# Sixty-one preferences in a planner's order of an attention and Fourier-mixing kernel

## The chip, the cores and the metric

One NeuronCore of a Trainium2 chip runs the whole kernel. The metric is the device time of one execution in microseconds; the median of three runs of the kernel before is 265.67 us (264.87 to 266.83). The profile is of a single execution with a span of 263.2 us.

## The reference

Two parts follow each other. The first is attention over q, k, v of 4 batches, 8 heads, 768 positions and 64 features, with 8 global keys, a causal window of 96 keys and a linear distance bias per head:

```python
scores = scale * np.matmul(q, k.transpose(0, 1, 3, 2))
is_global = pos[None, :] < int(n_global)
is_local = (rel >= 0) & (rel < int(n_local))
bias = -slopes[:, None, None] * dist[None, :, :]
scores = np.where(is_global | is_local, scores + bias, -1e9)
a = softmax(scores); out = a @ v
```

The heads are put side by side to x of shape (4, 768, 512), and the second part is

```python
X = np.fft.fft(np.fft.fft(x, axis=1), axis=2)
u = x + np.real(X)
un = (u - mu) / np.sqrt(var + 1e-06)          # over the last axis
return u + np.maximum(un @ w_ch1, 0.0) @ w_ch2
```

with w_ch1 of 512 x 2048 and w_ch2 of 2048 x 512. (Both are shortened here; names are the reference's.)

## The kernel before

The work is cut into units, and each unit is a function that emits instructions. A unit of TensorE is a group of matmuls into one PSUM bank or bank pair; what follows on the other engines (casts, exponentials, copies out of PSUM, folds, loads, stores) are single operations.

**Units of TensorE** stand in four lists. A unit's name is a pair (list, place).
- List 0, MIX, has ten units for each batch: four first transforms `py` (L979) of the folded attention output, three second transforms `pu` (L1059), and three transposes `ptu` (L1150) of normalized rows.
- List 1, ATT, has the attention. For batch 0: (1,0) ones, (1,1) transpose of the first head pair's q and k (`pt`, L575), (1,2) to (1,4) its scores (`sc`, a bias product L621 and a key product L633), (1,5) the placement of its values (`pvp`, L464, with a few idle matmuls, L457), then the same for further head pairs, global keys (`pgl`, L720) and the products with values (`pav`, L757 and L768). Batch 1 begins at (1,34); (1,36) to (1,38), (1,41) to (1,43), (1,46) to (1,48) and (1,52) to (1,54) are its scores.
- List 2, PH, has 96 hidden-layer units `ph` (L1180), eight for each of 12 row groups; each reads a quarter-share of w_ch1.
- List 3, PG, has 85 output-layer units (`pg` L1204 for eight row groups, `pgA` and `pgD` L1285, with fewer products, for the last four).

A score's bank is emptied by an exponential on ScalarE (`ex`, L657; in batches 2 and 3 `er`, L654, and a product on VectorE, L669). The global scores' exponential (`eg`, L733) adds a table `gb`. q and k are cast by L403, L405 or L407 on ScalarE, VectorE or GpSimd, values by L448 on GpSimd. The values placed in PSUM are copied out half by VectorE (L482) and half by ScalarE (L483). Weights are loaded and cast by eight issues on GpSimd's queue (L1464, L1469), each with a tile of the two weight matrices; the tiles' space holds q and k of batch 1 before. `py` is copied out by L994 and L996, mirrored by GpSimd (L1014 to L1016 and L1027), and `pu` is added to the residual on VectorE (L1078, L1087). Rows are normalized by L1109 or L1111, their squares summed by L1118.

**The order** is decided while the program is built, by `Plan`. It keeps a planned time for each engine, for each value and for each bank, from costs written in the file (`act`, `dve`, `pool`, `mm_us`), with landing times of some loads given as floors (`LAND`). Again and again it looks at the operations that are ready and at the next ten units of lists 0 and 1 and the next unit of lists 2 and 3, takes what can start first, and emits it. So each engine gets one fixed queue, in the order of emission, and runs it strictly in that order; the planned times are not in the program. A value `("qkT", n)` or `("h", c, jp)` is named by the operation that gives it. The candidate's key is its earliest start plus `BIAS`:

```python
c = (max(r, self.t["PE"]) + self.BIAS.get(name, 0.0), i, k, g or "", max(r, self.t["PE"]))
```

and `BIAS` is empty in this kernel. `first` (L112 on) has the same term for an operation, keyed by the first value that it gives. A unit that starts a bank takes the one that is free first: two pairs "xx", the pairs "C" and "D" in the first part, and two single banks each for `ph` and `pg` that take the place of C and D.

Of the kernel before, what the change touches and what calls it, by code (L numbers as in the profile page):

```python
# [22 lines left out]
class Plan:  # L23
# [62 lines left out]
    def first(self):  # L86

        best = None
        for i, (ready, p) in enumerate(self.ready):
            if p[11]:  # L90
                ready = [max(r, self.lanes[p[11] - 1]) for r in ready]
            c = (min(max(self.t[w[0]], r) for w, r in zip(p[1], ready)) - self.AHEAD * (p[10] < 0) + self.BIAS.get(p[4][0] if p[4] else None, 0.0),
                 p[10], ready[0], p[0], i)
# [45 lines left out]
        return tag  # L139

    LOOK = 10
    BIAS = {}
    AHEAD = 0.0

    def run(self, streams):

        left = [[(*u, (i, k)) for k, u in enumerate(s)] for i, (s, _) in enumerate(streams)]
        while True:
            best = None
            for i, s in enumerate(left):  # L150
                for k, (needs, ring, _, name) in enumerate(s[:self.LOOK if streams[i][1] else 1]):
# [11 lines left out]
                    else:  # L163
                        g = None
                    c = (max(r, self.t["PE"]) + self.BIAS.get(name, 0.0), i, k, g or "", max(r, self.t["PE"]))
                    if best is None or c < best:
# [15 lines left out]
def mm_us(n, k=1):  # L182
    return k * max(n / 2400.0 + 0.0025, 0.029)


def act(n):
    return 0.06 + n / 1200.0
# [15 lines left out]
def kernel(  # L203
# [45 lines left out]
    t1 = np.zeros((P, 4, 384))  # L249
# [11 lines left out]
    t2 = np.zeros((P, 4, 3, P))  # L261
# [10 lines left out]
    gb = np.zeros((64, 1))  # L272
# [15 lines left out]
    pl = Plan()  # L288
# [9 lines left out]
    def bank(tag, name, dtype=FP32):  # L298
        if tag in ("C", "D"):
            return early["pool"].tile([P, 2, 512 if dtype == FP32 else 1024], dtype, tag=tag, name=name, bufs=1)  # L300
        if tag == "xx":
            return ps.tile([P, 2, 512 if dtype == FP32 else 1024], dtype, tag=f"{tag}{tag.k}", name=name, bufs=1)
        if "late" not in early:
            early["ctx"].__exit__(None, None, None)
            early["late"] = ctx.enter_context(tc.tile_pool(name="psl", bufs=1, space=bass.MemoryType.PSUM))
        return early["late"].tile([P, 512], FP32, tag=f"{tag}{tag.k}", name=name, bufs=1)
# [5 lines left out]
    def free(tag, i):  # L312
        i -= NBUF[tag]
        return [("free", tag, i)] if i >= 0 else []
# [10 lines left out]
    sid = kon.tile([P, H, P], FP16, tag="sid", name="sid")  # L325
# [10 lines left out]
    kG = [kon.tile([P, HP, 32], FP16, tag=f"kG{i}", name=f"kG{i}") for i in range(2)]  # L336
# [165 lines left out]
    def BANKS(b):  # L502
        return ("xx", "C", "D") if b < 2 else ("xx",)

    def CD(b, ring):
        if b == 1 and ring in ("C", "D"):
            pl.left[("CD",)][0] += 1
            return [("CD",)]
        return [("CD",)] if b == 0 else []

    def RA(b):
        return 2 if b else 0
# [190 lines left out]
    def glob(b, halves):  # L703

        ns = [HP * b + 2 * half + i for half in halves for i in range(2)]
        needs = [("qkT", n) for n in ns] + [("kG", n, s) for n in ns for s in range(2)]

        def run(start, ring):
            pg = bank(ring, f"pgl_{b}_{halves[0]}")
            for half in halves:  # L710
                for i in range(2):
                    hp = 2 * half + i
                    if b >= FB:
                        for x in range(2):
                            nc.tensor.matmul(pg[32 * half:32 * half + 32, 0, x * 256:(x + 1) * 256].rearrange("p (a t m) -> p a t m", a=2, t=2),
                                             kG[b % 2][:, hp, :],
                                             TT[HP * b + hp][:, 0].rearrange("p (i t a m) -> p i a t m", t=2, a=2, m=64)[:, x + 1],
                                             start=(i == 0), stop=(i == 1), tile_position=(0, 32 * half), skip_group_check=True)
                        continue
                    nc.tensor.matmul(pg[32 * half:32 * half + 32, 0, :], kG[b % 2][:, hp, :],  # L720
                                     TT[HP * b + hp][:, 0, 256:S], start=(i == 0), stop=(i == 1),
                                     tile_position=(0, 32 * half))
            e = pl.pe(mm_us(512, 2 * len(halves)), start, True)
            for half in halves:
                pl.tok[("gldone", b, half)] = e
            for n in ns:
                pl.used(("free", "qkT", n), e)
            rows = slice(32 * halves[0], 32 * halves[-1] + 32)

            def ex():  # L730
                if ("free", "eg", b) not in pl.left:
                    pl.users(("free", "eg", b), 8)
                A(EG[rows], pg[rows, 0, :], AF.Exp, gb_sb[rows], 0.125)  # L733
            pl.later([("ACT", act(512), ex)], free("eg", b), e, [("eg", b, half) for half in halves], CD(b, ring), ring=ring, rank=RA(b))
        ATT.append((needs, BANKS(b), run))

    X = {}
# [654 lines left out]
    with tc.manual_schedule():  # L1392
# [12 lines left out]
        z = Ring("xx")  # L1405
# [188 lines left out]
```

## Time and profile before

| | before |
|---|---|
| median of three runs | 265.67 us |
| span of the profile | 263.2 us |
| PE busy | 244.6 us |
| VectorE busy | 176.6 us |
| ScalarE busy | 147.0 us |
| GpSimd busy | 68.0 us |
| first `ph` matmul | 52.26 us |
| last weight's landing seen by the store `hold` (L1478) | 68.67 us |
| last matmul ends | about 259.7 us |

Busy times are shares of one span, so an engine that is busy 93% on the whole can have a stage in which it waits much. The chain of work that ended last runs through VectorE, ScalarE, GpSimd and loads up to about 50 us and almost only through PE after it; PE makes up 73% of it. The page has 40 slices, so each digit stands for 6.58 us.

### The profile page before, as it was taken

How to read it: one execution, taken by the hardware profiler on the slowest of the kernel's cores; microseconds unless marked ns; L12 is line 12 of the kernel's file. 1: busy time of each engine (PE TensorE's matmuls, PEld its weight loads, DVE VectorE, ACT ScalarE, POOL GpSimd, SP SyncE). 2: the span in 40 equal slices, each digit the busy share in tenths (PEclk: the TensorE clock that was granted, in tenths of full speed). 3: DMA queues.
4: the chain of work that ended last, by engine and by line, in shares of the span. 5: the costliest groups of instructions: out<-in, count | busy, mean ns of one | idle time of the engine just before them, and what ended most of it. 6: DMA issues, size and time to landing. Idle time of an engine off the chain costs nothing.

```text
span 263.2 us, 7311 instructions
## 1 busy us (share of the span) xinstructions
PE 244.6 (93%) x3080; PEld 179.5 (68%) x3080; DVE 176.6 (67%) x360; ACT 147.0 (56%) x249; POOL 68.0 (26%) x133
## 2 busy tenths in 40 slices
PE   8687678799999999999999999999999999999994
PEld 3555555687856876775685565679777668888883
DVE  4568997752599756661398968677998734644463
ACT  1467878776476467963861454995346164533300
POOL 1445398652020525123100523021001410010000
PEclk9999999799999999999999999999999999999999
DMA  7999969999599993995999896502071331310222
GB/s 217 295 289 307 312 175 246 216 215 206 119 202 292 239 195 90 219 230 101 232 159 191 248 232 131 133 0 42 9 194 79 82 80 40 83 40 2 80 79 82
DMA packets 76386, 42.02 MB, mean 160 GB/s; under 512 B 33474, under 2 KB 72514, under 8 KB 76354
## 3 DMA queue, kind: packets, MB, share of 16 engines
q1 hardware_dynamic: 69298, 32.65, 55.6%
q0 software_dynamic: 4224, 4.19, 9.5%
q10 hardware_dynamic: 2832, 4.72, 6.6%
q8 instruction: 24, 0.39, 0.6%
q14 instruction: 8, 0.07, 0.1%
HBM read 31.59 MB, written 9.44 MB: 156 GB/s over the span
## 4 chain that ended last, share of the span: by engine, by line
PE 73%; DVE 11%; ACT 5%; POOL 3%; issue 3%; DMA 3%; SPq 1%; POOLq 0%; ACTq 0%
PE ph L1180 29%; PE pg L1204 17%; PE pgD L1285 5%; PE pgA L1285 4%; PE pav L768 3%; PE pu L1059 3%; PE py L979 3%; DMA u<-in_v_dram 3%; PE sc L630 2%; POOL ww L1027 2%; ACT ex L657 2%; DVE x L788 2%; PE pav L757 1%; SPq L399 1%; PE ptu L1150 1%
## 5 line engine op out<-in xcount | busy, mean ns | idle before, releaser
L1180 PE MATMUL ph<-unT,w 128*128 128x256 f16 x768 | 93.5, 273 | 0.0
L1180 PEld LDWEIGHTS <-w 128*128 128x128 f16 x768 | 72.9, 98 | 13.7 <-issue 2.6
L1186 ACT ACTIVATE hT<-ph 128x512 f16<-128x512 f32 x78 | 46.2, 598 | 46.5 <-PE ph L1180 44.7
L1204 PE MATMUL pg<-w,hT 128*128 128x512 f16 x256 | 60.0, 379 | 0.0
L1204 PEld LDWEIGHTS <-hT 128*128 128x128 f16 x256 | 24.3, 98 | 24.6 <-issue 0.7
L657 ACT ACTIVATE ex<-sc 128x992 f16<-128x992 f32 (+2 forms) x24 | 20.6, 933 | 7.2 <-PE sc L633 7.1
L654 ACT ACTIVATE er<-sc 128x992 f16<-128x992 f32 (+2 forms) x24 | 21.6, 929 | 4.5 <-PE sc L630 4.3
L1213 DVE SCALAR_TENSOR_TENSOR u<-pg,sm,u 128x512 f32<-128x512 f32 x16 | 11.9, 746 | 12.9 <-PE pg L1204 12.8
L669 DVE TENSOR_TENSOR ex<-er,mk 128x992 f16<-128x992 f16 (+2 forms) x24 | 15.5, 645 | 7.3 <-ACT er L654 7.0
L1027 POOL COPY ww<-zy 128x512 f16<-128x512 f16 x16 | 10.0, 652 | 29.9 <-PE py L979 29.9
L1125 POOL TENSOR_SCALAR sm<-sm 128x2 f32<-128x2 f32 x12 | 2.5, 211 | 57.1 <-ACT un L1118 54.8
L768 PEld LDWEIGHTS <-ex 128*128 128x128 f16 x352 | 14.9, 97 | 2.5 <-issue 1.8
L1187 DVE TENSOR_SCALAR hT<-ph 128x512 f16<-128x512 f32 x18 | 12.4, 689 | 6.1 <-PE ph L1180 5.9
L1118 ACT ACTIVATE un<-un 128x512 f16<-128x512 f16 x24 | 15.0, 629 | 2.4 <-DMA unT<-un 1.9
L768 PE MATMUL pav<-v,ex 128*128 128x65 f16 x352 | 16.1, 193 | 0.2 <-ACT v L483 0.2
L403 ACT ACTIVATE qk<-qs 128x768 f16<-128x768 f32 x11 | 9.3, 844 | 12.1 <-DMA out_dram<-u 7.2
L1109 ACT ACTIVATE un<-u,sm 128x512 f16<-128x512 f32 x16 | 11.2, 718 | 8.2 <-DVE sm L1082 8.2
L1078 DVE SCALAR_TENSOR_TENSOR u<-pu,xr 128x512 f32<-128x512 f32 x18 | 11.7, 687 | 4.0 <-PE pu L1059 3.8
L493 POOL CAST v<-qs 128x768 f16<-128x768 f32 x8 | 6.7, 832 | 28.1 <-DMA qs<-in_v_dram 28.1
L1285 PEld LDWEIGHTS <-hT 128*128 128x128 f16 x128 | 12.5, 98 | 1.6
L788 DVE TENSOR_TENSOR x<-pav,rc 128x512 f16<-128x512 f32 (+1 forms) x21 | 12.9, 615 | 0.7
L536 POOL COPY kG<-qkT 64x8 f16<-64x8 f16 x32 | 9.8, 308 | 10.8 <-DVE qkT L586 8.1
(122 smaller groups left out, 379.3 us busy)
## 6 DMA issues: line engine op xcount, KB each, us to landing
out_dram<-u SPq DMA_DIRECT2D x23, 256.0 KB, 2.4
w<-in_moe_w_ch_dram POOLq DMA_DIRECT2D x8, 512.0 KB, 19.0
qs<-in_q_dram SPq DMA_DIRECT2D x9, 384.0 KB, 5.8
qs<-in_k_dram SPq DMA_DIRECT2D x9, 384.0 KB, 5.4
qs<-in_v_dram SPq DMA_DIRECT2D x16, 192.0 KB, 5.4
xr<-xd ACTq DMA_DIRECT2D x3, 768.0 KB, 5.9
u<-in_v_dram SPq DMA_DIRECT2D x5, 384.0 KB, 7.2
w<-in_q_dram SPq DMA_DIRECT2D x4, 384.0 KB, 6.5
```

The lines of the kernel that those rows point to most:

```text
L654: A(mine(), cut(pa), AF.Exp, 0.0, 0.125)
L657: A(cut(expst[hp][:, :, g * 512:g * 512 + (384 if g == 2 else 512)]), cut(pa), AF.Exp, 0.0, 0.125)
L669: VT(o, mine(), m, op=ALU.mult)
L768: nc.tensor.matmul(po[:, jj, hh * 65:(hh + 1) * 65], lhsT, v16[b % 2][:, i, h, 0:65], start=(jp == 0 and a == 0), stop=(a == len(ops) - 1) ...
L788: VT(X[b][:, 2 * jp:2 * jp + 2, first * Dh:(first + nh) * Dh].rearrange("p j (h d) -> p j h d", d=Dh), pv[:, :, :, 0:Dh], rc.to_broadcast( ...
L1027: nc.gpsimd.tensor_copy(rev[:, n], T[("y", b)][:, n, :, :, ::-1])
L1118: A(x, x, AF.Square, accum_out=MV[c][:, a, 2:3])
L1180: nc.tensor.matmul(ph[:, a * CH:(a + 1) * CH].rearrange("p (x m) -> p x m", x=2), W1[0][:, d, jb * P:(jb + 1) * P], UNT[c][:, :, d, :], st ...
L1186: pl.later([("ACT", act(512), lambda: A(dst, ph, AF.Relu)), ("DVE", dve(512), lambda: V.tensor_scalar_max(dst, ph, 0.0))], [], e, [("h", c ...
L1187: ("DVE", dve(512), lambda: V.tensor_scalar_max(dst, ph, 0.0))],
L1204: nc.tensor.matmul(pg, HT[c][:, jb, t * P:(t + 1) * P], W2[0][:, jb, :], start=(jb == 0), stop=(jb == NJ - 1))
L1285: nc.tensor.matmul(o, lhs(j), rhs(j), start=(first and j == 0), stop=(j == NK - 1), skip_group_check=True)
```

## The change

`BIAS` gets 61 entries. A negative number makes the planner take that unit or operation earlier, as if it could start so many microseconds sooner, a positive one later. The values were found by trying one after the other in the plan, and the trial counted pauses of TensorE too. Nothing else of the program's work is altered: a unit has the same instructions, only the order on each engine and the choice of the bank or (where an operation may run on two engines) of the engine follow from it. The second edit names the load of the bias table `gb` as a need of the global exponential, so that the planner may not put the load behind it when it moves things.

```diff
@@ -139,7 +139,15 @@
         return tag
 
     LOOK = 10
-    BIAS = {}
+    BIAS = {(1, 5): -0.7, ('ss', 1, 1): -3, (2, 27): -0.7, ('ex', 1, 3, 2): -3, (1, 46): -0.7, ('qk', 10, 1): -1.5, ('c', 't1'): 1.5, ('w1', 2): 3,
+            ('er', 4): -0.7, ('ss', 2, 0): 0.7, ('h', 6, 6): 3, ('qk', 5, 0): 3, ('qkT', 6): -0.7, ('c', 't2'): 0.3, ('ex', 1, 2, 0): -0.7,
+            ('xb', 11, 2): -1.5, ('h', 6, 5): 3, ('ss', 2, 1): 0.7, ('qkT', 10): -0.7, ('ex', 0, 2, 1): -1.5, (3, 13): 0.7, (1, 42): 0.7,
+            ('un', 7, 0): -0.7, ('s', 11, 3): 0.7, ('x', 0, 3, 2): -1.5, ('qk', 9, 0): 1.5, ('qk', 7, 1): -0.7, ('qk', 0, 0): 1.5,
+            ('ld', 15, 1): 1.5, ('h', 5, 1): 0.3, ('h', 5, 4): 0.3, ('qk', 11, 1): 0.7, (3, 73): -1.5, ('un', 0, 1): -1.5, ('y', 1, 2, 0): 3,
+            ('er', 2): 0.3, ('qkT', 8): 0.7, ('h', 8, 4): -1.5, ('w1', 0): 3, ('vc', 2): 0.7, (1, 36): 0.3, (3, 47): 0.3, ('ld', 8, 1): -1.5,
+            ('ob', 11, 1): -3, ('qkT', 14): 0.7, ('er', 19): -0.3, ('h', 8, 0): -1.5, (1, 92): -0.7, ('kG', 14, 0): 0.3, ('u', 5, 0): 0.3,
+            ('w2t', 0): 0.3, ('z', 3, 0): 3, (1, 64): -1.5, ('v', 0, 2, 0): -0.3, ('ss', 6, 1): 3, (2, 21): -1.5, (2, 19): 0.3, ('rd', 10, 0): -0.7,
+            ('sid', 2): -0.3, (3, 51): -3, (2, 5): -3}
     AHEAD = 0.0
 
     def run(self, streams):
@@ -731,7 +739,7 @@
                 if ("free", "eg", b) not in pl.left:
                     pl.users(("free", "eg", b), 8)
                 A(EG[rows], pg[rows, 0, :], AF.Exp, gb_sb[rows], 0.125)
-            pl.later([("ACT", act(512), ex)], free("eg", b), e, [("eg", b, half) for half in halves], CD(b, ring), ring=ring, rank=RA(b))
+            pl.later([("ACT", act(512), ex)], free("eg", b) + [("c", "gb")], e, [("eg", b, half) for half in halves], CD(b, ring), ring=ring, rank=RA(b))
         ATT.append((needs, BANKS(b), run))
 
     X = {}
```

In the order that comes out, among other things:
- On PE, the value placement (1,5) stands before the scores (1,2) to (1,4); (1,36) and (1,42) stand among `py` and `pu` of batch 0.
- ScalarE begins with the two casts of the first q and k, and casts more of batch 1's q and k, which GpSimd or VectorE did; it also has the copy `qkT` 5, which was VectorE's.
- GpSimd issues the first two weight loads behind the last key copies of batch 1, and the other six behind the mirrors of batch 0 and a cast of values.
- SyncE issues the two transform tables `t1` and `t2` behind batch 1's q and k.
- At the end, VectorE adds the full row of the last group before the first half row.

## The prediction

> **What bounds the kernel now.** I read the page first (share of each engine, then the slices), then busy time by stage, then the order of instructions inside the stages with pauses.
>
> ```profile
> PE 244.6 (93%) x3080; PEld 179.5 (68%) x3080; DVE 176.6 (67%) x360; ACT 147.0 (56%) x249; POOL 68.0 (26%) x133
> ...
> PE   8687678799999999999999999999999999999994
> ...
> PEclk9999999799999999999999999999999999999999
> ```
>
> TensorE is the bound, but not everywhere: the first eight slices (6.6 us each) are 6 to 8 tenths busy, the rest full, and in slice 8 the granted clock dips. By stage (columns: PE, PEld, DVE, ACT, POOL busy us; clock; DMA):
>
> ```profile
> 0.00:20.00 20.00, 15.14 (x356) 9.48 (x356) 11.09 (x36) 8.99 (x12) 6.67 (x20) 1.00 1.05 267
> 20.00:44.00 24.00, 17.35 (x543) 12.58 (x544) 21.70 (x49) 20.06 (x29) 16.15 (x26) 1.00 0.99 263
> 44.00:52.30 8.30, 6.32 (x131) 5.25 (x131) 5.50 (x15) 6.04 (x16) 5.30 (x10) 0.82 1.19 216
> 52.30:259.70 207.40, 205.75 (x2056) 152.16 (x2052) 137.82 (x266) 111.92 (x196) 39.91 (x77) 1.00 0.65 136
> ```
>
> From the first hidden-layer product (52.3) to the last matmul, PE is idle for 207.40 - 205.75 = 1.65 us. A reordering can't take more than that from 207 us; PE's work there is the same before and after. Before 52.3 it is idle 4.9 + 6.7 + 2.0 = 13.5 us. So the question is when the product `ph` starts. From 20 to 44 VectorE is the fullest (21.7 of 24), ScalarE next (20.1): a serial fold on VectorE feeds the transforms `py`, then `pu`, then `ph`.
>
> One second at a time, clock column last but two:
>
> ```profile
> 49.00:50.00 1.00, 0.98 (x48) 0.92 (x47) 0.85 (x5) 0.78 (x3) 0.94 (x2) 0.65 1.18 218
> 50.00:51.00 1.00, 1.00 (x12) 1.00 (x11) 0.97 (x2) 1.00 (x3) 0.31 (x1) 0.50 1.19 216
> 51.00:52.00 1.00, 1.00 (x30) 0.72 (x32) 0.37 (x1) 1.00 (x4) 0.00 (x0) 0.50 1.19 215
> 52.00:53.00 1.00, 1.00 (x21) 0.79 (x22) 1.00 (x5) 0.59 (x4) 0.28 (x2) 0.64 1.19 215
> ```
>
> For about 3.4 us the clock is half. In the three us before it PE was busy only 0.29, 0.64 and 0.32.
>
> **What the Trainium skill says.** "TensorE: Matmul & The Clock Gate", section "What's actually happening": an activity monitor halves the clock after a mostly idle window of about 3.4 us, and the window runs freely. The trace agrees in length (49.3 to 52.7) and cause. "ScalarE: Activation LUTs", "What ACT_TABLE_LOAD costs": about 1283 ns; the trace has one load, 1283 ns, and "Table sets: the hidden batching unit" says copies are in every set, so casts ahead of the first exponential should need no second load (the built order holds one). "SBUF — State Buffer", "Who interferes with whom": VectorE and GpSimd exclude each other on a shared port pair. The trace fits: one L839 takes 1.04 us under a GpSimd cast against 0.42 elsewhere.
>
> **The change, by parts.** No arithmetic is added or removed: the same units, each engine in another order. I worked from the built order of both kernels and the durations above.
>
> *The table.* The bias table `gb` stays ninth on SyncE's queue; the added need costs nothing, since the first global exponential (16.88) runs about 9 us after that load's issue at 7.12.
>
> *Start: a loss.* In the kernel before:
>
> ```profile
> 8.08 2.56 ACT L657 ACTIVATE ex<-sc 128x992 f16<-128x992 f32 x3 [4.95 <-PE sc L633]
> ...
> 8.26 0.82 POOL L448 CAST v<-u 128x768 f16<-128x768 f32 x1
> ...
> 9.13 0.36 PE L464 MATMUL pvp<-v,ident 64*64 64x128 f16 x12 [0.37 <-POOL v L448]
> ...
> 9.43 0.95 PE L457 MATMUL pvp<-eg 128*128 128x128 f16 x14
> ...
> 10.42 0.56 DVE L482 CAST v<-pvp 128x384 f16<-128x384 f32 x1 [0.36 <-PE pvp L457]
> ...
> 11.02 0.49 ACT L483 ACTIVATE v<-pvp 128x384 f16<-128x384 f32 x1 [0.37 <-DVE v L482]
> ```
>
> The changed order puts placement of values (1,5) ahead of the three score units of the first head pair. They queue on PE behind a wait for the value cast, so they start at about 10.3 instead of 6.84, and ScalarE, which takes that placement's copy first, starts `ex` at 11.4 instead of 8.08. Its three exponentials free the banks for the next transpose: second one ends at 11.4 + 2 x 0.85 = 13.1, transpose 13.1 instead of 10.7/11.8 (halves), delay 1.4. The two first casts, also moved to ScalarE (844 ns against 560), end by 7.2 and hide behind the value load. Next, the copy of (1,18)'s values on ScalarE now waits for VectorE's, which ran after it before: ScalarE is 1.9 us late at 23.7 (before 21.8).
>
> *20 to 44: the loss is won back.* ScalarE had pauses of 0.9 and 0.6 us there, and cast qk(5,0) (0.85) stood between the exponentials and `eg`; now qk(4,0) fills the pause. `eg` ends at 27.9 against 28.04. VectorE starts its fold at 25.5 against 24.22, but loses `qkT` 5 (0.95) to ScalarE (my estimate there 1.42: 1025 ns for 1024 elements, 631 for 512, extended to 1536) and, with one GpSimd cast fewer beside it, perhaps 0.5 to 1.0 of port waits: 42.6 + 1.3 - 0.95 - 0.75 = 42.2. `py` starts about as before (40.4), `pu` at 44.7 (before 44.56). Two score units (1,36), (1,42) are moved into the pauses of this stage.
>
> *44 to 52: the gain.* GpSimd before:
>
> ```profile
> 45.50 0.74 POOL L1469 DMA_DIRECT2D w<-in_moe_w_ch_dram  x1
> ...
> 48.15 0.81 POOL L448 CAST v<-qs 128x768 f16<-128x768 f32 x1
> 48.92 0.61 POOL L1027 COPY ww<-zy 128x512 f16<-128x512 f16 x1
> ```
>
> A weight issue and a cast stand between the mirror copies, and the last `pu` waits for the copy ending at 49.5. The changed order runs all mirrors first: 44.7 + 0.6 + 1.0 + 0.6 = 46.9. Then the second `pu` runs at 46.35 (47.36), the third at 47.25 (49.70). The normalized rows then set the pace on ScalarE: `un` 00 ends 48.6, copies and `un` 10, 11 follow to 50.7, transpose 0.57, `ph` at 51.3 (52.26). With `pu` at 44.7 to 48.2 PE is busy 80% of the window that was idle, so I expect no half clock: two `ph` units in 1.75 instead of 2.12. Gain 0.95 + 0.37 = 1.3.
>
> *Weights: risk.* Six of the eight weight issues move behind those copies, to 47.7 to 51.5 (before 38.2 to 45.5). From 36.6 to 68.7 (the store `hold`, waiting for the last weight, issues at 68.67) the DMA engines are full: over 36 to 70 the weight queue takes 73% of 34 us, 3.1 us a weight, the other queue 9.7. A full queue lands at the same end; third weight near 54, fourth 57, fifth 60, sixth 62.6. Needed: fifth hidden unit 55.5, seventh 57.8, first output unit 61.7, second 64.3. Margins 0.9 to 1.8 us: no cost in my value, up to 3 at the other bound.
>
> *After 52.* Same work on a full PE: I count 0.3 of the 1.65 idle as won. *Tail.* The last full-row addition (0.75) now precedes a half-row one (0.48, before in the shadow of PE), so the last addition, at 259.69 before, slips 0.2 to 0.5: +0.3.
>
> Sum: -1.3 - 0.3 + 0.3 = -1.3, **264.4 us**.
>
> **Rivals.** (1) *The late weights or the late start stay* (slower side): three weights each 1 us late, or the start's 1.4 not absorbed because ScalarE, with three more casts and a transpose copy (about 4 us), becomes the bound before `py`. 265.7 + 2 = 267.7. For: margins under 2 us, ScalarE 20.1 of 24. Against: ScalarE's pauses, DMA never idle. (2) *The pauses really go*: VectorE without port waits and ScalarE without gaps pull `ph` to 49, and the pauses after 52 halve: 265.7 - 3.5 = 262.2. For: 13.5 us idle. Against: VectorE's fold starts later. (3) *All cancels*, the start's loss against the half clock: 265.7.
>
> **How the numbers follow.** My forecast 0.40, rival 3 0.15, rival 2 0.27, rival 1 0.18. One percent is 2.7 us: faster 0.30 (rival 2 and the edge of mine), same 0.52, slower 0.18. Range: rival 2 less 0.7 to rival 1 plus 0.3, 261.5 to 268.
>
> **What would show it.** Right: first exponentials after 11 us, PE idle more in 6 to 13; no half clock near 50; third `pu` before 48; `ph` at about 51.3; span after it 208. Wrong: PE waiting for a DMA of `w` at 55 to 65; ScalarE without pauses and late `py`; a half clock elsewhere, at the start for instance, where PE now pauses for 1.5 us; new waits of PE after 60.

## The result and the profile after

The changed kernel takes 264.82 us (median of 20 runs, 262.83 to 266.11) beside 265.85 for the kernel before (20 runs); the ratio is 0.9957, interval 0.9937 to 0.9978. It is faster by 0.4%, in the range and 0.4 us above the forecast. Ratios, here and below, compare fast executions alone and differ by up to 0.15% from the quotients of the medians. The two traces show that most of the steps that led there were not what happened. (In the changed kernel's code, line numbers are 8 higher than before.) The page after:

```profile
PE 246.5 (93%) x3080; PEld 180.6 (68%) x3080; DVE 173.3 (66%) x355; ACT 151.4 (57%) x257; POOL 67.2 (25%) x130
...
PE   8678778799999999999999999999999999999993
...
PEclk9799999979999999999999999999999999999998
```

There are two dips of the clock now, in slices 2 and 9 (counted from 1), where there was one in slice 8 (the 8 in the last slice lies behind the last matmul). By stage, with the same columns as before:

```profile
0.00:20.00 20.00, 14.49 (x302) 8.58 (x302) 7.85 (x30) 9.25 (x12) 6.09 (x18) 0.91 1.05 267
20.00:44.00 24.00, 18.99 (x576) 13.56 (x576) 21.84 (x47) 21.38 (x31) 10.66 (x21) 1.00 0.95 256
44.00:52.30 8.30, 6.62 (x142) 5.15 (x134) 7.27 (x20) 6.67 (x15) 5.96 (x11) 1.00 1.18 225
```

The first stage has fewer of its matmuls done (302 instead of 356) and a clock of 0.91. The first `ph` begins at 53.07, which is 0.81 later than before and 1.8 later than forecast. What follows is shorter. Busy times from the first `ph` to the last matmul, first the kernel before, then the changed one:

```profile
52.26:259.66 207.40, 205.79 (x2060) 152.21 (x2052) 137.85 (x265) 111.96 (x196) 39.91 (x77) 1.00 0.65 136
```

```profile
53.07:259.69 206.62, 205.96 (x2062) 153.01 (x2052) 134.74 (x258) 113.37 (x200) 43.69 (x80) 0.99 0.68 136
```

PE idles 0.66 us there instead of 1.61. Its busy time is no less, but it holds 3.4 us at half clock (below), which cost up to 1.7. Behind the last matmul the span runs 4.0 us instead of 3.6. So in these two pages +0.81 - 0.78 + 0.42 makes the changed kernel 0.5 us *longer* (263.7 against 263.2), while the medians are 1.0 apart the other way: the profiled execution of before is 0.8 under its median, that of after 0.7 over its own. A difference of a third of a percent isn't read from one pair of pages.

**The start.** The order came out as worked out, and one thing on top:

```profile
9.32 0.53 PE L472 MATMUL pvp<-v,ident 64*64 64x128 f16 x12 [1.62 <-POOL v L456]
9.79 1.68 PE L465 MATMUL pvp<-eg 128*128 128x128 f16 x14
11.39 0.63 PE L629 MATMUL sc<-dist,sid 64*64 64x496 f16 x4
...
12.48 2.56 ACT L665 ACTIVATE ex<-sc 128x992 f16<-128x992 f32 x3
```

PE waits 1.62 us for the cast of values, its clock halves at 9.3, and the 14 filling matmuls that stand between the placement and the scores take 1.68 us instead of 0.95. The first exponentials start at 12.48, not at the forecast's 11.4 (8.08 before).

**The fold.** VectorE and GpSimd beside each other:

```profile
41.35 1.07 DVE L947 TENSOR_TENSOR ww<-eA 128x768 f16<-128x768 f16 x1
42.34 1.47 DVE L956 TENSOR_TENSOR eA<-zy 128x1536 f16<-128x1536 f16 x1
...
41.09 1.91 POOL L1431 COPY distk<-dist 64x640 f16<-64x640 f16 x2
```

The same two operations took 0.55 and 0.95 before. They are stretched exactly while GpSimd copies the distance table of the later batches, which the new order put there. The fold ends at 44.73 (42.60 before; 42.2 forecast).

**The rows ahead of the first `ph`.** ScalarE:

```profile
48.31 0.97 ACT L665 ACTIVATE ex<-sc 128x960 f16<-128x960 f32 x1 [1.56 <-PE sc L641]
49.18 0.29 ACT L1107 ACTIVATE sm<-sm 128x1 f32<-128x1 f32 x2
49.50 1.34 ACT L1117 ACTIVATE un<-u,sm 128x512 f16<-128x512 f32 x2
```

From 48.31 to 52.77, where the last row copy `un` ahead of `ph` ends, ScalarE does one thing after another, and PE's transposes wait for it (0.83 and 0.33 us). The exponential of the added score unit (1,42) stands ahead of the first normalized row.

**The clock near 54.** One second at a time:

```profile
51.00:52.00 1.00, 0.34 (x32) 0.33 (x30) 1.00 (x3) 1.00 (x3) 1.00 (x2) 1.00 1.29 306
52.00:53.00 1.00, 0.50 (x32) 0.38 (x31) 1.00 (x4) 1.00 (x4) 1.00 (x2) 1.00 1.00 179
53.00:54.00 1.00, 1.00 (x24) 0.78 (x13) 0.89 (x2) 1.00 (x5) 1.00 (x3) 0.84 1.19 203
54.00:55.00 1.00, 1.00 (x6) 0.75 (x5) 0.55 (x1) 1.00 (x5) 1.00 (x2) 0.50 1.24 201
```

After two microseconds at 0.34 and 0.50 busy, the first `ph` units run at half clock, from 53.7 to 57.1.

**The end.** VectorE's last additions:

```profile
258.85 0.75 DVE L1311 SCALAR_TENSOR_TENSOR u<-pgA,sm,u 128x512 f32<-128x512 f32 x1 [1.39 <-PE pgA L1293]
259.73 0.88 DVE L1311 SCALAR_TENSOR_TENSOR u<-pgD,sm,u 128x256 f32<-128x256 f32 x2
```

Two quarters in a row (0.88) stand behind the last matmul, where before there was one (0.48).

### The profile page after: what moved, and what is told of

Same layout as the page of the kernel before. It is cut to its first block, busy times and chain, and to the rows that moved or that the text cites. A ratio compares the mean times of both kernels' runs of the same rounds, so it can differ in the third digit from the quotient of the medians.

```text
span 263.7 us, 7306 instructions
## 1 busy us (share of the span) xinstructions
PE 246.5 (93%) x3080; PEld 180.6 (68%) x3080; DVE 173.3 (66%) x355; ACT 151.4 (57%) x257; POOL 67.2 (25%) x130
## 4 chain that ended last, share of the span: by engine, by line
PE 77%; ACT 10%; DVE 5%; DMA 2%; issue 1%; POOL 1%; SPq 1%; DVEq 0%
PE ph L1188 30%; PE pg L1212 21%; PE pgD L1293 5%; ACT ex L665 4%; PE pgA L1293 4%; PE pav L776 4%; PE pu L1067 3%; PE py L987 3%; DMA u<-in_v_dram 2%; PE sc L638 2%; DVE qkT L594 2%; ACT er L662 2%; PE pav L765 1%; ACT un L1117 1%; POOL ww L1035 1%
## 5 line engine op out<-in xcount | busy, mean ns | idle before, releaser
L1188 PE MATMUL ph<-unT,w 128*128 128x256 f16 x768 | 94.7, 276 | 0.0
L1188 PEld LDWEIGHTS <-w 128*128 128x128 f16 x768 | 73.9, 99 | 13.9 <-issue 2.2
L1194 ACT ACTIVATE hT<-ph 128x512 f16<-128x512 f32 x81 | 48.1, 599 | 48.4 <-PE ph L1188 48.3
L662 ACT ACTIVATE er<-sc 128x768 f16<-128x768 f32 (+2 forms) x24 | 21.4, 929 | 6.0 <-PE sc L638 5.9
L677 DVE TENSOR_TENSOR ex<-er,mk 128x768 f16<-128x768 f16 (+2 forms) x24 | 15.6, 661 | 8.1 <-ACT er L662 7.9
L1133 POOL TENSOR_SCALAR sm<-sm 128x2 f32<-128x2 f32 x12 | 4.4, 368 | 62.8 <-ACT un L1126 62.6
L1035 POOL COPY ww<-zy 128x512 f16<-128x512 f16 x16 | 9.2, 609 | 21.1 <-PE py L987 17.7
L1195 DVE TENSOR_SCALAR hT<-ph 128x512 f16<-128x512 f32 x15 | 10.3, 688 | 6.1 <-PE ph L1188 6.0
L1117 ACT ACTIVATE un<-u,sm 128x512 f16<-128x512 f32 x13 | 9.2, 720 | 8.7 <-DVE sm L1090 8.5
L544 POOL COPY kG<-qkT 64x8 f16<-64x8 f16 x32 | 8.1, 256 | 18.9 <-DVE qkT L594 15.0
```

The lines of the kernel that those rows point to most:

```text
L662: A(mine(), cut(pa), AF.Exp, 0.0, 0.125)
L677: VT(o, mine(), m, op=ALU.mult)
L1035: nc.gpsimd.tensor_copy(rev[:, n], T[("y", b)][:, n, :, :, ::-1])
L1188: nc.tensor.matmul(ph[:, a * CH:(a + 1) * CH].rearrange("p (x m) -> p x m", x=2), W1[0][:, d, jb * P:(jb + 1) * P], UNT[c][:, :, d, :], st ...
L1194: pl.later([("ACT", act(512), lambda: A(dst, ph, AF.Relu)), ("DVE", dve(512), lambda: V.tensor_scalar_max(dst, ph, 0.0))], [], e, [("h", c ...
```

## Experiments

Apart from e5 and e7, each kernel plays back a list of decisions, the emission order on all engines, so that only what the diff names is moved; all compute the whole result. Medians of the kernel before beside them: 265.31 (e1 to e4), 265.39 (e5 to e8), 265.50 (e9 to e11) and 265.32 (e12).

**Which part of the order gains?** Three kernels join the two orders at a unit of PE.

```diff
 # e1
-order = changed
+order = before up to unit (2,0), the first ph; then changed
 # e2
+order = changed up to unit (2,0); then before
 # e3
+order = before up to and with attention unit (1,13); then changed
```

> The order is given as a list: everything up to the first hidden unit as in the kernel before, everything after it as in the changed kernel. Theory A (the gain lies after the start of ph: fewer waits and fewer switches of TensorE between small and full tiles, about 1.8 us, and the first part of the change loses about 0.8): ph starts near 52.3, the stage from there to the last matmul takes about 205.5 instead of 207.4, time 264.0. Theory B (my prediction: the gain lies before ph): time as before, 265.6 to 265.9.

> The other half of the swap: the changed order up to the first hidden unit, the order of before after it. Theory A: ph starts near 53, the later stage takes 207 plus what a half clock there costs, time 266.7. Theory B: ph starts at 51.3 to 52, time 264.5.

> The changed order, but its start as before: all up to the third transpose (1,13) in the order of before (scores ahead of the value placement, first casts on VectorE). Theory A: no half clock near 10 us, first exponentials at 8.1, ph 1 to 2 us earlier than in the changed kernel, time 263.3. Theory B (the start's loss is won back before 44 us): ph as in the changed kernel, time 264.8.

Measured: e1 263.6 us, ratio 0.9952 (0.9928 to 0.9976). e2 266.12, ratio 1.0036 (1.0015 to 1.0057): the changed head alone makes the kernel slower. e3 263.91, ratio 0.995 (0.9926 to 0.9975), first exponentials at 7.96 and first `ph` at 52.32. e1 and e2 go with theory A: the gain lies behind the first `ph`, and the head, which the forecast held for the gain, is a loss. e3 goes with it in the profile, 0.75 us earlier at the first `ph`; its time lies between the two theories and is not apart from the changed kernel's. In the profile of e2 the stretch behind the first `ph` is 207.87 us, about as long as in the kernel before (207.40), though its waits fall elsewhere (one of 1.3 us for values is new). The profiled execution of e1 is 2.3 us over its median and misses the expected 52.3: GpSimd waits 1.05 us for a load of values, the half clock lasts 6.8 us instead of 3.4, and the first `ph` is at 53.80. From there to the last matmul it takes 206.29 us, with 2.7 us of half clock among them.

**Why is the fold late?**

```diff
 # e4: GpSimd
-... weight issues 1, 2; dist_k copies; mirrors; v cast; weight issues 3 to 8
+... weight issues 1, 2; mirrors; v cast; weight issues 3 to 8; dist_k copies
```

> The changed order with GpSimd's two copies of the distance table moved from beside VectorE's fold (41 to 43 us) to behind the weight issues. If the port shared by the two engines stretches the fold: L947 back to 0.56 and L956 to 0.95, fold 1.0 us earlier, time 263.8. If the transforms wait for ScalarE's exponentials (their banks) instead: fold earlier, ph at the same time, 264.8.

Measured: 264.18 us, ratio 0.997 (0.9951 to 0.9989). The time alone is between the two theories and not apart from the changed kernel's; the profile decides. VectorE in e4 (its lines are 167 higher):

```profile
40.70 0.55 DVE L1114 TENSOR_TENSOR ww<-eA 128x768 f16<-128x768 f16 x1
41.17 0.95 DVE L1123 TENSOR_TENSOR eA<-zy 128x1536 f16<-128x1536 f16 x1
```

Both are back at their length without the GpSimd copy, so the stretching was the two engines in each other's way. It cost 0.52 + 0.52 = 1.04 us of the fold. The first `ph` came at 52.26, 0.81 earlier than in the changed kernel's profile, but the start has a part in that: in e4 the half clock began 0.9 later and the first exponentials are at 11.72 instead of 12.48. Beside e2, which has the same head up to these copies and its exponentials at 11.69, what the copies cost at the first `ph` is 0.42 us (52.68 in e2). The stretching agrees with the Trainium skill, "SBUF — State Buffer", section "Who interferes with whom" (VectorE and GpSimd lock each other out of a shared port pair).

**Does the half clock near 54 belong to the order? Are changes of tile form dear? What does the start cost? What does the tail?** Four kernels on one chip.

```diff
 # e5: the changed kernel, no edit
 # e6: after (3,2), ten times
-narrow narrow wide wide
+narrow wide narrow wide
 # e7
-            if n == 1:
-                idle(10)
+            if n < 2:
+                idle(10 if n else 22)
...
-            if n == 0:
-                idle(14)
 # e8: VectorE at the end
-half row; PE's last 8 matmuls; quarter; quarter
+half row; quarter; PE's last 8 matmuls; quarter
```

> The changed kernel itself, once more, to stand on the same chip beside the next three. Both theories: 264.8 us, 0.4% below the kernel before. It also asks whether the half clock near 54 us that its first profile shows belongs to the order: if it does, it is there again; if it falls where the chip's count happens to lie, it may be gone, and PE's last matmul then ends about 1.5 us earlier than 259.7.

Measured: 264.33 us, ratio 0.9948 (0.9927 to 0.997). In its profile PE is as little busy in the microseconds before 53 (0.27 and 0.56), and the clock stays full: the half clock near 54 doesn't belong to the order alone (the last section says on what it hangs). The one at the start does: it is there again, from 11.0 to 14.4. The first `ph` is at 53.0. One weight comes late here: a `ph` waits 0.48 us for it at 57.8.

> From the projections of the first sequence on, ten pairs of narrow units followed by two wide ones are taken apart (narrow, wide, narrow, wide), so that TensorE goes between small-tile and full units 82 times after the first ph instead of 64; the same matmuls, no other edit. Theory S (each change between narrow and wide costs TensorE about 0.1 us, and the six fewer of the changed order are a part of its gain after 52 us): 18 x 0.1 = 1.8 us later than the changed kernel, 266.6. Theory W (only waits count; a switch is free): the changed kernel's time within 0.4 us, 264.8.

Measured: 266.15 us, ratio 1.0024 (1.0004 to 1.0045), 1.8 later than e5: theory S. Wide units use the whole 128 by 128 array, narrow ones a part of it. In the expectation the product with values counts as narrow, though it runs on the full 128 by 128 array. Counted by the form of the tile, the changes after the first `ph` are 54 in the kernel before, 51 in the changed one and 66 here. So 15 more changes; busy time from the first `ph` to the last matmul:

```profile
53.46:260.55 207.09, 205.97 (x2061) 151.16 (x2052) 135.01 (x258) 113.40 (x200) 41.94 (x80) 1.00 0.63 135
```

e5 is busy 204.60 in that stretch, also at full clock: 1.37 / 15 = 0.09 us for each (0.11 against e7's 204.34). So 1.4 of the 1.8 is the changes; that the whole agrees with theory S's 18 x 0.1 is in part luck. PE in a part of it:

```profile
107.13 1.05 PE L1356 MATMUL ph<-unT,w 128*128 128x256 f16 x8
108.11 0.39 PE L806 MATMUL sc<-qkT 64*128 64x256 f16 x4
108.44 1.05 PE L1356 MATMUL ph<-unT,w 128*128 128x256 f16 x8
```

From their start to that of the score behind them, eight `ph` take 0.98 us here; in the changed kernel sixteen take 1.85 up to the next unit of another form (115.64 to 117.49), so sixteen in two halves take 0.11 more. The Trainium skill says in "TensorEngine Tiling (Array Packing)", section "Key Properties", that a change of the tiling mode drains TensorE; it gives no time, and here it is about 0.1 us.

> The changed kernel with the 14 filling matmuls of the first value placement moved: none behind it, and 22 ahead of it, where TensorE waits 1.6 us for the cast of v. Theory P (the start is late because the pause brings the half clock, and because the fill stands between the placement and the first scores): full clock from 8 to 13 us, first exponentials at about 10.3 us instead of 12.5, and of the 2 us about 1 is left at the first ph: 263.9. Theory Q (what is lost at the start is absorbed by 44 us anyway, as the prediction had it): first exponentials earlier, the time as the changed kernel, 264.8.

Measured: 263.84 us, ratio 0.9934 (0.9906 to 0.9961). The start:

```profile
9.64 0.36 PE L472 MATMUL pvp<-v,ident 64*64 64x128 f16 x12 [0.80 <-POOL v L456]
...
11.03 2.56 ACT L663 ACTIVATE ex<-sc 128x992 f16<-128x992 f32 x3
```

The clock is full until 37.2 (where a stretch at half clock follows another pause), and the exponentials come 1.45 earlier, not the 2.2 expected: ScalarE's own copy of the values stands ahead of them. Of the 1.45, 0.66 is left at the first `ph` (52.41). The 0.5 us under e5 is within the intervals; the places in the profile go with theory P, with smaller sizes.

> The changed kernel with one thing of its tail as before: the addition of the last pair's first quarter and its store stand ahead of the pair's other half instead of behind it. Theory T (the prediction's: two quarter additions in a row behind the last matmul are the loss): the last addition ends 0.4 us sooner and the time is 264.4. Rival: the stores behind the last addition set the end in either order: 264.8.

Measured: 265.09 us, ratio 0.9985 (0.9965 to 1.0005). The edit put the quarter behind the half row, which was not meant, and PE's last eight matmuls, which go into the bank that the quarter is read from, waited 1.23 us for it. Neither theory was tried by this; e9 has the order that was meant.

**The tail again, and the losses undone together.**

```diff
 # e9: VectorE at the end, as before
-half row; PE's last 8 matmuls; quarter; quarter
+quarter; PE's last 8 matmuls; half row; quarter
 # e10 = changed + e4 + e7 + e9
 # e11 = e3 + e4 + e9
```

> The changed kernel with the whole end of its VectorE list as before: the last pair's first quarter and its store, then the last eight matmuls, then the pair's other half, then the last quarter (the try before put the quarter behind the half, and TensorE waited 1.2 us for it). Theory T (the prediction's: two quarters in a row behind the last matmul are the loss): no new wait of TensorE, the last addition is one quarter instead of two, the span ends 3.5 us after the last matmul instead of 4.0, and the time is 264.1 against the changed kernel's 264.6. Rival: the stores set the end in either order, 264.6.

Measured: 264.21 us, ratio 0.995 (0.9934 to 0.9967). VectorE:

```profile
258.36 0.75 DVE L1479 SCALAR_TENSOR_TENSOR u<-pgA,sm,u 128x512 f32<-128x512 f32 x1 [0.39 <-PE pgA L1461]
259.23 0.48 DVE L1479 SCALAR_TENSOR_TENSOR u<-pgD,sm,u 128x256 f32<-128x256 f32 x1
```

The last matmul ends at 259.19 and the span at 262.8, 3.6 us later instead of 4.0: theory T in the profile, too little to be seen in the times.

> The changed kernel with three things undone at once: the fill ahead of the first value placement, the two table copies behind the weights' issues, the end of VectorE's list as before. Theory A (each is a separate loss: 0.7, 0.5 and 0.4 us): 263.0 or below, first exponentials at 11.0 us, the folds at 0.55 and 0.95 us, first ph at about 51.7, the span's end 3.5 us after the last matmul. Rival O (the first two overlap, since ScalarE's exponentials set the middle in either case): 263.5 or more, first ph at 52.3 as with either alone.

> The kernel before's order up to the first pair's thirteenth attention unit (so its start, first exponentials at 8 us), then the changed order, with the two table copies behind the weights' issues and the end of VectorE's list as before. Theory A (start, tables and tail are separate losses): 262.9, below the kernel before by 1% and below the changed kernel by 0.6%. Rival O: the start's and the tables' parts overlap, 263.6; the first ph stays at 52.3.

Measured: e10 264.24 us, ratio 0.9945 (0.9919 to 0.9971); e11 263.36, ratio 0.9927 (0.99 to 0.9955). The first `ph` is at 52.08 and 52.07, hardly before e4's 52.26 or e7's 52.41: rival O. The start's loss and the fold's lie on two ways to the same `ph`, and ScalarE's exponentials set it when both are mended: the fold ends at 42.69 in e10 and at 43.33 in e11, but the second `py` starts at 43.44 and 43.42, after a wait of 0.24 us for `ex` in each. In both profiles the clock is full up to the last matmul and the span 261.2. e11 is the fastest of all by its median, 0.7% under the kernel before; its interval overlaps the changed kernel's, so that it beats that one is likely and not shown.

**Fewer changes of form still?**

```diff
 # e12 = e11, after (3,2), four times and one more narrow unit moved to the next
-narrow wide narrow wide
+narrow narrow wide wide
```

> The version with the kernel before's start, late table copies and tail as before, and with five narrow units moved next to a neighbour so that TensorE goes between narrow and wide units 58 times after the first ph instead of 64. Theory S (0.1 us each, as the ten pairs taken apart showed in the other direction): first ph at 52.1 us as there, from it to the last matmul 0.6 us less than the 205.3 us of that version, so about 204.7, and a time of 262.8. Rival: the units moved together wait for a score bank or for ScalarE, TensorE's waits after 53 us grow from 0.8 to 1.4 us or more, and the time stays at 263.4.

Measured: 268.25 us, ratio 1.0112 (1.0074 to 1.0149): the rival, and worse than it. PE's waits after 53 us:

```profile
PE pu L1234 <- POOL ww L1202: 1.0, 1, 1.0
PE pav L932 <- DVE x L963: 1.0, 2, 0.7
PE sc L805 <- ACT er L829: 0.9, 1, 0.9
PE pu L1234 <- ACT zy L1169: 0.7, 2, 0.5
```

From the first `ph` to the last matmul it takes 210.48 us against 205.51 in e11. PE's idle time is 2.7 us more (3.69 against 0.97), and a half clock from 52.4 to 55.8 cost up to 1.7. That leaves 0.6, although the saved changes should have won 0.2. These 0.8 us are waits too, which the idle time doesn't show: measured from start to start, as in the next section, PE's waits are 5.5 us against 2.0 in e11.

## Why the prediction came out near, and where it was wrong

*The table*: right. The first global exponential follows ScalarE's work before it without a wait (19.38).

*Start: a loss*: right in its mechanism, too small. The casts ahead of the first exponential brought no second table load, as expected: the trace has one, of 1283 ns. The forecast has `ex` at 11.4, the trace 12.48. What is missing is that the pause, which it saw, brings the half clock on the placement, the fill and the scores; it stands only among the signs of a wrong forecast. The profiles agree without exception: with the pause (changed, e2, e4, e5, e6, e8, e9) a half clock begins between 8.7 and 11.0 us; with the pause filled (e7, e10) or with the start of before (before, e1, e3, e11, e12) none comes before 18. Nor is the loss won back later: in the six profiles with this head (changed, e2, e5, e6, e8, e9) the first exponentials come between 11.69 and 14.04 us and the first `ph` between 52.68 and 54.59, in the same order.

*20 to 44: the loss is won back*: this step failed. `eg` ends at 29.4 instead of 27.9, the fold at 44.73 instead of 42.2. The estimate for `qkT` 5 on ScalarE held (1.45 against 1.42). The fold was to win 0.5 to 1.0 by a cast less on GpSimd; it lost 1.04 to the copies of the distance table, which the order moved beside it (e4). The other 1.1 us of its delay came from earlier: the last part of the fold begins at 39.88 instead of 38.79. I had looked at what left GpSimd there and not at what came.

*44 to 52: the gain*: the mirrors do run together. From the first `pu` to the third it takes 3.38 us instead of 5.14 (forecast 2.55), and from the first `pu` to `ph` 7.08 instead of 7.70 (forecast 6.6). So 0.6 was gained of the forecast's 1.1, but the first `pu` is 1.4 late (45.99 against 44.56). "No half clock" failed in the profiled execution (one begins at 53.7) and held in e5; the pauses that may bring it, 0.34 and 0.50 busy before 53, are still there, since PE waits for ScalarE's rows. The 0.37 for two `ph` units was too much in any case: it set 2.12, which runs to the drawn end of the last matmul, against 1.75, which runs from start to start. At full clock the same sixteen matmuls are drawn 1.92 us long (e2), so 0.2 was to be had.

*Weights*: right, with margins as thin as said: no wait for a weight in the changed kernel's profile, 0.48 us in e5's, 0.3 in e4's, none in the others'.

*After 52: 0.3*: the mis-sized term, and the source of the gain. In six profiles of the changed order with full clock there (e4, e5, e7, e9, e10, e11) it takes 205.0 (e7) to 206.2 us (e4) from the first `ph` to the last matmul; the kernel before takes 207.4, of which 0.2 is half clock. So the term is 1.0 to 2.2. The step that failed is its bound: PE is idle for 1.65 us there, and "a reordering can't take more than that". In these traces idle time isn't all of PE's waiting. The kernel before:

```profile
85.83 1.58 PE L1180 MATMUL ph<-unT,w 128*128 128x256 f16 x13
87.95 1.03 PE L979 MATMUL py<-t,ww 128*128 128x256 f16 x8 [0.55 <-DVE zy L996]
```

A `ph` matmul is drawn 0.27 us long, but where nothing waits the next one starts 0.11 us after it. So `py` could have started at 85.83 + 13 x 0.109 = 87.25. It is 0.70 late, and only 0.55 of that shows as idle: some 0.16 us of every wait behind a `ph` lies under the drawn end of the matmul before it, and a shorter wait doesn't show at all. An estimate from the starts of all matmuls (each distance less the one that the same two kinds of matmul have where nothing waits) gives waits of 3.3 us behind the first `ph` in the kernel before and 4.0 in e2, against 1.5 in the changed kernel's first profile and in e7, 2.0 in e11 and 2.6 in e5 with its late weight. Idle time shows in seven places there in the kernel before, in two after. When waits, half clock and 0.094 us for each change of tile form are taken off, 198.7 to 198.8 us are left in all fourteen profiles. So PE's work is the same, as the prediction said, and the gain is waits (0.6 to 1.8 us at full clock) and three changes of form fewer (0.3).

*Tail*: right, +0.4 in the profile.

The forecast was -1.0 by `ph` at 51.3, -0.3 for two `ph` units at full clock, -0.3 after and +0.3 at the end. The runs show +0.8, -1.0 to -2.2 at full clock, and +0.4: a sum of 0.2 to -1.0, beside -1.0 by the medians. The rest is within what single pages scatter (0.7 and 0.8 from their medians here). The mean clock is 0.988 over 29 executions of the changed kernel and 0.9945 over 144 of the kernel before: one more stretch of 3.4 us at half clock in a typical execution, and the one at the start, which the +0.8 already holds, is that long. So the forecast came near because two errors cancel, a head that isn't won back and a later stage that wins three to seven times as much, and not by its argument. Rival 1 had the late start, rival 2 the halved pauses after 52; none had both.

## What to carry to other kernels

A planner's order moves what no edit names: for each stage that is to gain, list what comes onto every engine beside it as well as what leaves, above all on GpSimd beside a chain of VectorE. A pause of TensorE costs more than its length when it brings a half clock onto what a later stage waits for, and matmuls that fill it belong ahead of the work that is waited for, not behind. When TensorE is 99% busy, its idle time is no bound on what an order can win: waits lie under the drawn ends of matmuls, so compare the distances of their starts. Count changes of tile form too, but merging units to save them is worth it only where the moved units' consumers have slack (0.09 us each here, against waits of 0.5 to 1).

## What the runs showed of the hardware

- A change between a full matmul and a 64 by 128 tile costs about 0.09 us of TensorE (e6). The starts show it directly, for other tiles too: in e2 and e11 the next matmul starts 0.11 us after a `ph` when it is another `ph`, and 0.20 us after it when it is a `sc` (64 by 128), a `pvp` (64 by 64) or a `pvg` (128 by 32).
- In a trace a `ph` matmul is drawn 0.27 us long and the next starts 0.11 us after it, so TensorE's busy time holds up to 0.16 us of each wait (the kernel before at 87.95).
- VectorE's operations with two f16 inputs (TENSOR_TENSOR) of 768 and 1536 elements took 1.07 and 1.47 us beside a GpSimd copy of 640 elements, 0.55 and 0.95 alone (e4).
- A stretch at half clock lasted 3.4 us, or 6.8 (e1, e8, e9), each time it came; e10 and e11 had none up to the last matmul. At the start it began between 2.2 us before the end of the pause (e8, where the pause was 3.1 us long) and 1.0 us after it (e5). The Trainium skill, "TensorE: Matmul & The Clock Gate", "What's actually happening", speaks of a window that runs freely, and the runs agree. Cut every execution into stretches of 3.41 us, counted from its own changes of the clock: of the stretches at full clock, all nine with PE busy for 0.45 or less were followed by half clock, none with more than 0.61 was, and in between 5 of 19 were. The pause ahead of the first `ph` falls into one stretch in the changed kernel's first profile (50.27 to 53.68, busy 0.61, half clock after it) and is shared by two in e5 (0.75 and 0.86, none).
